# Two f steps of a dense layer in one PSUM bank, with one 512-column activation chain, and an attention operand rebuilt without copies across partitions

## Chip, cores and metric

One core of a Trainium2 chip. The metric is the device time of one execution in microseconds (us); for the kernel before it is the median of three runs. PE is TensorE, DVE VectorE, ACT ScalarE, POOL GpSimd and SP SyncE, which here only issues DMAs.

## The reference, cut to what matters

```python
def reference(q, k, v, n_sink, window, moe, moe2):        # q, k, v: 4 x 8 x 768 x 64
    scores = matmul(q, k.T) / sqrt(64)                     # sliding window of 128 keys and 4 sink keys
    x = matmul(softmax(where(keep, scores, -1e9)), v)      # -> x: 3072 tokens x 512
    h = x @ w_in                                           # first layer: 512 -> 2048
    x = (h - tanh(h)) @ w_out                              # 2048 -> 512
    logits = x @ w_gate + modality_bias[modality_id]       # second layer: 8 experts, one a token
    e = argmax(logits)
    out = gate[e] * (relu(x @ w1[e]) @ w2[e])
```

All in fp32. The kernel computes most products with matmul operands of the type fp32r, in which a number is carried as two parts: hi (the number rounded by a cast) and lo (the number less hi). A product then takes three matmuls, hi·hi, hi·lo and lo·hi.

## The kernel before, in words

The 3072 tokens are worked in 12 **chunks** c of 256. A chunk has 8 **units** U of attention (one per head, 96 in all); the first 14 units (`nf=14`) run in plain fp32, the others with split operands. The first layer ("the first MoE" of the change's description, although it is dense) has 16 **f steps** a chunk, each for 128 of its 2048 inner columns. After it the chunk is routed, and when all chunks are done the second layer runs over 13 pages of 256 tokens of one expert each (the lines from L720 on, `m_...`).

Everything runs in one interleaved stream: while PE works on the first layer of chunk c, the attention of chunks further on is fed in between. The order comes from `run_chunks` (L831): every piece of work is an event with a planned time in units of one f step, `emit` sorts the events, and Tile's scheduler then orders the instructions of each engine, starting from that list. The offsets stand in `self.o` (L45): `lag` (L2's delay behind L1 of the same f), `tg` (gact's delay), `ts` (a_split's) and so on.

The pieces that matter here:

- **L1** (L164): 12 matmuls of 128x256 into one PSUM tile h of one f step. The h tiles come from a pool of two PSUM banks (512 fp32 columns each; before, 256 of them are used).
- **gact** (L177): from h the value g = h − tanh(h), as h·h²·(polynomial in h²). On ACT u = h² (L184) and y = (K1·u + K0)² (L185), on DVE z = u·h (L188) and z = (y + KC)·z (L194), and on ACT a Relu of u whose running sum in `over` (L189) tells whether h ever left the polynomial's range. In that case the whole computation is redone by `general` and `gact_any`, which does not happen with these inputs.
- **g_split** (L197): hi = cast of z on ACT (L211), lo = z − hi on POOL (L216). The tile g holds both.
- **L2** (L237): 6 matmuls of 128x512 for every f step, with the two halves of g as weights, into the accumulators acc0 and acc1, one PSUM bank each.
- **a_split** (L292): from the loaded q (128 partitions x 256: q's 64 rows twice) the operand A = [hi; lo], the upper 64 partitions holding hi and the lower lo. POOL makes the lower half in place (L300, printed as `A<-q,A`, with `sub`'s line L216), then two DMAs on SP's queue copy the halves of A crosswise into B = [lo; hi] (L301, L302). K = [hi; lo] likewise, its lower half by DVE. The scores (L314, L315) are A·K + B·K, in which all four products appear.
- **a_splitv** (L283): V's hi on ACT, its lo on POOL (`V<-v,V`).
- **r_route** (L656): at the end of each chunk POOL issues two indirect DMAs which scatter the gates and token numbers of 2 x 128 tokens into the DRAM table xs (`xs<-pl,sl`).
- **r_order** (L662): after the last chunk but one and after the last, some 20 small DVE operations decide in which order the pages of the second layer run. Their result is the tile `order`; SP reads it and then issues the loads of the pages' weights (L726, `mr<-in_moe_w_dram`) and tokens.

The lines that matter to the change, as they stand:

```python
nc.scalar.activation(u, h, AF.Square)
nc.scalar.activation(y, u, AF.Square, bias=self.k0, scale=K1)
nc.vector.tensor_mul(z, u, h)
nc.vector.scalar_tensor_tensor(out=z, in0=y, scalar=KC, in1=z, op0=ALU.add, op1=ALU.mult)
...
self.sub(self.e("qlo", U < 16), A[D:], q[D:], f32(A[D:]))
nc.sync.dma_start(f32(Bt[:D]), f32(A[D:]))
nc.sync.dma_start(f32(Bt[D:]), f32(A[:D]))
```

Of the kernel before, what the change touches and what calls it, by code (L numbers as in the profile page):

```python
# [40 lines left out]
class Kern:  # L41
    def __init__(self, tc, a):
        self.tc, self.nc, self.a = tc, tc.nc, a
        self.Wi, self.Wo = {}, {}
        self.o = dict(tc='a', xa='g', mt0=-0.28, gz='v', mxe=11, lx='v', nf=14, efh='a', trc=-14.17, tpf=-1.86, xhi='v', vhi='a', vlo='g', qhi='a', khi='v', sT='a', tr='a', ev='a', glo='g', whi='a', wlo='g', gk=0, wl=-8.54, wls=1.25, wd=-3.86, wds=1.05, wo=1, bs=2, be=3, bE=3, bV=1, bg=2, btr=1, bxt=1, pt={'h': 'h', 's': 'r', 'T': 'r', 'R': 'R', 'x': 'R', 'Q': 'R'}, pb=(('r', 2), ('h', 2), ('R', 2)), tl=-9.97, ts=-5.86, tv=-4.34, tsv=-2.34, tS=-5.24, dS=0.07, tN=-4, dN=0.5, tT=-1.78, dT=0.35, tPV=-0.39, txs=-0.28, tg=0.64, tre=0.05, trl=0.48, trr=3.39, u0=-15.64, g=2, lag=1.96, raw=2, sp=2, ghi='a', qlo='g', klo='v', eh='v', xlo='v', x2=4, me=13, mxl=8.77, mxt=1.5, mlag=1.45, mwl=9.99, mws=3.27, mm=0, ev0='v', ghi0='a', vhi0='a', sT0='a', qhi0='a', xlo0='g', eh0='v', y=2)  # L45
# [130 lines left out]

    def gact(self, c, f):  # L177

        nc = self.nc
# [10 lines left out]
        if self.e("gz", c == 0) == "g":  # L190
            nc.scalar.activation(y, y, AF.Identity, bias=self.kc)
            nc.gpsimd.tensor_mul(z, y, z)
        else:
# [24 lines left out]
    def gact_any(self, c, f):  # L218

        nc = self.nc  # L220
        h = self.h.pop((c, f))[:, :CH]
# [1 line left out]
        u = g.tile([P, CH], F32, tag="u", name=f"u{c}_{f}")
        t = g.tile([P, CH], F32, tag="z", name=f"t{c}_{f}")
        y = g.tile([P, CH], F32, tag="y", name=f"gy{c}_{f}")
        m = g.tile([P, CH], U8, tag="m", name=f"m{c}_{f}")
# [777 lines left out]
```

## Time and profile before

| what | value |
|---|---|
| median of 3 runs (lowest to highest) | 1222.81 us (1222.67 to 1223.86) |
| the profiled execution, its device time | 1225.8 us |
| its span in the trace | 1224.0 us |
| mean granted clock of TensorE, share of full speed | 0.96 |
| busy share of PE, DVE, ACT, POOL | 93%, 72%, 62%, 54% |
| DMA: mean rate, packets | 121 GB/s, 88256 |

The profile is of one execution. The span runs from its first to its last recorded instruction, and the device time has 1.8 us more. "Busy" is the time in which an engine worked on instructions; the remaining time it waited, or issued something that isn't counted. In the rows of groups and of the timelines, `<-ENGINE tile` after an idle time names what ended it. The granted clock is the share of the full 2.4 GHz at which the chip let TensorE run in a stretch (0.5 is its lower level, 1.2 GHz).

### The profile page before, as it was taken

Reading aid. Unit: us, or ns where it says so; the run is one execution under the profiler, and the core shown is the slowest. Engines: PE = TensorE matmul, PEld = TensorE weight load, DVE = VectorE, ACT = ScalarE, POOL = GpSimd, SP = SyncE. Lnnn points to the kernel's source line nnn. Section 1 sums busy time; section 2 is a strip of 40 time slices with the busy share of each in tenths; the row PEclk is TensorE's granted clock in tenths of the full one; section 3 lists DMA queues with packets and bytes.
Section 4 is the critical chain, followed back from the end, with each engine's and each line's share of the span. In section 5 each row is a group of like instructions: output and inputs, shape, how many; then the busy total and the mean of one; then the engine's idle time right before and its main releaser. Section 6 shows DMA issues by size and latency. Waiting matters only on the chain. (4 is left out here: it accounts for less than half of the span.)

```text
span 1224.0 us, 23714 instructions
## 1 busy us (share of the span) xinstructions
PE 1135.9 (93%) x7171; PEld 994.8 (81%) x7171; DVE 885.5 (72%) x2419; ACT 757.4 (62%) x2123; POOL 657.7 (54%) x973
## 2 busy tenths in 40 slices
PE   7879998999899899999899999999798999999993
PEld 3447787988789789989789988988687989999992
DVE  6889896888778687978778887966647566666720
ACT  3445765777577678767577877775726555555620
POOL 4987865777667668767667767763302211211200
PEclk9859998999999899999999999999998999999997
DMA  7654232333323233333333323200909777777500
GB/s 206 203 187 137 75 91 62 102 80 102 60 76 90 71 88 85 98 69 104 60 91 83 104 66 87 81 12 19 343 19 327 238 226 213 222 241 219 168 26 6
DMA packets 88256, 147.98 MB, mean 121 GB/s; under 512 B 18864, under 2 KB 64432, under 8 KB 88112
## 3 DMA queue, kind: packets, MB, share of 16 engines
q1 hardware_dynamic: 83184, 133.16, 37.2%
q0 software_dynamic: 4928, 13.14, 3.0%
q8 instruction: 61, 1.00, 0.4%
q14 instruction: 83, 0.68, 0.2%
HBM read 122.86 MB, written 13.17 MB: 111 GB/s over the span
## 5 line engine op out<-in xcount | busy, mean ns | idle before, releaser
L172 PE MATMUL h<-xt,wi 128*128 128x256 f32 x2304 | 356.1, 290 | 9.9 <-DVE gz L188 9.0
L246 PE MATMUL acc<-wo,g 128*128 128x512 f32 x1152 | 334.5, 407 | 24.0 <-POOL g L216 23.1
L172 PEld LDWEIGHTS h<-xt,wi 128*128 128x128 f32 x2304 | 320.5, 194 | 40.4 <-DVE gz L188 12.4
L246 PEld LDWEIGHTS acc<-wo,g 128*128 128x128 f32 x1152 | 198.6, 192 | 53.1 <-POOL g L216 26.0
L216 POOL TENSOR_TENSOR g<-gz,g 128x256 fp32r<-128x256 f32 x192 | 153.4, 802 | 82.3 <-ACT g L211 78.4
L735 DVE TENSOR_TENSOR ml<-mr,mh 128x1024 fp32r<-128x1024 f32 x104 | 127.9, 1236 | 53.4 <-ACT mh L734 51.8
L778 PE MATMUL mh<-mxt,mh 128*128 128x256 f32 x832 | 157.9, 286 | 3.2 <-DVE mxt L768 2.5
L795 PE MATMUL macc<-mh,mg 128*128 128x512 f32 x416 | 147.9, 401 | 4.3 <-DVE mg L782 4.3
L778 PEld LDWEIGHTS mh<-mxt,mh 128*128 128x128 f32 x832 | 138.1, 193 | 12.1 <-DVE mxt L768 2.9
L189 ACT ACTIVATE u<-u,kt 128x256 f32<-128x256 f32 x192 | 97.8, 509 | 80.2 <-DVE gz L188 73.8
L355 POOL TENSOR_SCALAR_AFFINE_SELECT X<-fl 128x512 fp32r<-128x512 f32 (+1 forms) x192 | 119.2, 643 | 33.6 <-DVE fl L385 24.5
L804 POOL DMA_INDIRECT out_dram<-mo,mi x26 | 28.5, 1096 | 200.2 <-ACT mo L803 196.0
L734 ACT CAST mh<-mr 128x1024 fp32r<-128x1024 f32 x104 | 108.6, 1052 | 40.9 <-PE macc L795 25.2
L188 DVE TENSOR_TENSOR gz<-u,h 128x256 f32<-128x256 f32 x192 | 78.9, 414 | 57.5 <-POOL g L216 34.2
L778 PE MATMUL mh<-mxt,ml 128*128 128x256 f32 x416 | 118.5, 286 | 0.0
L194 DVE SCALAR_TENSOR_TENSOR gz<-gy,gz 128x256 f32<-128x256 f32 x192 | 108.3, 570 | 9.2 <-ACT gy L185 2.7
L328 ACT ACTIVATE e<-e,nm 128x160 f32<-128x160 f32 x192 | 82.0, 427 | 48.0 <-DVE nm L326 46.5
L211 ACT CAST g<-gz 128x256 fp32r<-128x256 f32 x192 | 77.0, 402 | 44.4 <-DVE gz L194 29.7
L337 POOL TENSOR_SCALAR e<-e,sm 128x160 f32<-128x160 f32 x192 | 96.9, 515 | 11.6 <-DVE sm L332 9.6
L216 POOL TENSOR_TENSOR A<-q,A 64x256 fp32r<-64x256 f32 x82 | 69.4, 846 | 56.3 <-issue 14.0
L781 ACT ACTIVATE mg<-mh 128x256 fp32r<-128x256 f32 x104 | 40.3, 387 | 94.2 <-PE mh L778 88.3
L185 ACT ACTIVATE gy<-u,k 128x256 f32<-128x256 f32 x192 | 96.5, 510 | 2.5
(211 smaller groups left out, 2270.5 us busy)
## 6 DMA issues: line engine op xcount, KB each, us to landing
mr<-in_moe_w_dram SPq DMA_DIRECT2D x104, 512.0 KB, 4.7
k<-in_k_dram SPq DMA_DIRECT2D x82, 224.0 KB, 2.7
v<-in_v_dram SPq DMA_DIRECT2D x96, 128.0 KB, 2.3
q<-in_q_dram SPq DMA_DIRECT2D x82, 128.0 KB, 2.2
B<-A SPq DMA_DIRECT2D x164, 64.0 KB, 2.1
rawi<-in_moe_w_in_dram SPq DMA_DIRECT2D x16, 512.0 KB, 5.7
rawo<-in_moe_w_out_dram SPq DMA_DIRECT2D x16, 512.0 KB, 5.6
x2d<-x SPq DMA_DIRECT2D x24, 256.0 KB, 2.2
```

Of the source, the lines that this page charges most:

```text
L172: nc.tensor.matmul(h[:, :CH], w[:, wl, k * P:(k + 1) * P], x[:, xl, k], start=(n == 0), stop=(n == 11))
L185: nc.scalar.activation(y, u, AF.Square, bias=self.k0, scale=K1)
L189: nc.scalar.activation(u, u, AF.Relu, bias=self.kt, accum_out=self.over[:, n:n + 1])
L194: nc.vector.scalar_tensor_tensor(out=z, in0=y, scalar=KC, in1=z, op0=ALU.add, op1=ALU.mult)
L216: (self.nc.vector if eng == "v" else self.nc.gpsimd).tensor_tensor(out=out, in0=a, in1=b, op=ALU.subtract)
L246: nc.tensor.matmul(o, g[:, gl, t * P:(t + 1) * P], w[:, wl], start=(f == 0 and n == 0), stop=(f == NF - 1 and n == 2))
L337: self.nc.gpsimd.tensor_scalar(out=e, in0=e, scalar1=r, scalar2=1.0, op0=ALU.mult, op1=ALU.mult)
L355: self.nc.gpsimd.affine_select(out=out, in_=in_, pattern=[[0, n], [s, P]], base=0, channel_multiplier=-s, compare_op=ALU.is_gt if prev els ...
L734: nc.scalar.copy(hi, r)
L735: nc.vector.tensor_sub(lo, r, f32(hi))
L778: nc.tensor.matmul(h, w[:, k * P:(k + 1) * P], x[:, xl, k], start=(n == 0), stop=(n == 11))
L795: nc.tensor.matmul(self.macc[g][t], gt[:, gl, t * P:(t + 1) * P], w[:, DM:], start=(f == 0 and n == 0), stop=(f == n8 - 1 and n == 2))
```

## The change

Three things change.

1. **A pair of f steps shares a bank.** L1 of an even f takes an h tile and fills its columns 0 to 255, L1 of the odd f after it fills columns 256 to 511. gact runs once for the pair, at 512 columns, planned at the odd step's time plus `tg`. z gets no tile of its own: u·h is written over h in PSUM, and (y + KC)·h goes into y. u has one buffer instead of two. g is one tile of 512 columns for the pair, `over` has half the columns, and gact_any is changed in the same way.
2. **`lag` goes from 1.96 to 3.4**, so L2 of every f step, and what is planned behind it (the evacuation of the accumulators, the routing), is planned 1.44 steps later.
3. **a_split without copies.** A stays [hi; hi], and POOL writes lo = q − hi over all 128 partitions of B = [lo; lo]. The two DMAs a unit are gone (164 of them in all). A·K is then hi·hi + hi·lo and B·K is lo·hi + lo·lo.

```diff
@@ L1
+        if f % 2 == 0:
+            self.h[c, f // 2] = self.ps("h", F32, f"h{c}_{f}")
+        h = self.h[c, f // 2][:, (f % 2) * CH:(f % 2 + 1) * CH]
...
@@ gact, now called with p = f // 2
-        u = g.tile([P, CH], F32, tag="u", name=f"u{c}_{f}")
-        y = g.tile([P, CH], F32, tag="y", name=f"gy{c}_{f}")
+        u = g.tile([P, 2 * CH], F32, tag="u", name=f"u{c}_{p}", bufs=1)
+        y = g.tile([P, 2 * CH], F32, tag="y", name=f"gy{c}_{p}")
         nc.scalar.activation(u, h, AF.Square)
         nc.scalar.activation(y, u, AF.Square, bias=self.k0, scale=K1)
-        z = g.tile([P, CH], F32, tag="z", name=f"gz{c}_{f}")
-        n = c * NF + f
-        nc.vector.tensor_mul(z, u, h)
+        n = c * (NF // 2) + p
+        nc.vector.tensor_mul(h, u, h)
         nc.scalar.activation(u, u, AF.Relu, bias=self.kt, accum_out=self.over[:, n:n + 1])
...
-            nc.vector.scalar_tensor_tensor(out=z, in0=y, scalar=KC, in1=z, op0=ALU.add, op1=ALU.mult)
-        self.g_split(c, f, z)
+        nc.vector.scalar_tensor_tensor(out=y, in0=y, scalar=KC, in1=h, op0=ALU.add, op1=ALU.mult)
+        self.g_split(c, p, y)
@@ g_split
-        gt = self.gp.tile([P, 2, CH], F32R, tag="g", name=f"g{c}_{f}", bufs=self.o["g"])
+        gt = self.gp.tile([P, 2, 2 * CH], F32R, tag="g", name=f"g{c}_{p}", bufs=self.o["g"])
@@ L2
+            q = (f % 2) * CH + t * P
-                nc.tensor.matmul(o, g[:, gl, t * P:(t + 1) * P], w[:, wl],
+                nc.tensor.matmul(o, g[:, gl, q:q + P], w[:, wl],
@@ a_split
         self.cast(self.e("qhi", U < 16), A, q)
-        self.sub(self.e("qlo", U < 16), A[D:], q[D:], f32(A[D:]))
-        nc.sync.dma_start(f32(Bt[:D]), f32(A[D:]))
-        nc.sync.dma_start(f32(Bt[D:]), f32(A[:D]))
+        self.sub(self.e("qlo", U < 16), Bt, q, f32(A))
@@ run_chunks
-                    add(t + f + self.o['tg'], self.gact if banded else self.gact_any, c, f)
+                    if f % 2:
+                        add(t + f + self.o['tg'], self.gact if banded else self.gact_any, c, f // 2)
@@ self.o: lag=1.96 becomes lag=3.4
```

How the order moves, at three places. Lines are those of the kernel in question; a name's number after the last underscore tells nothing.

**POOL, the end of chunk 0's first layer and its scatter** (g1_6 and g1_4 are gact's result for f step 6, or now pair 4, of chunk 1; A23 and B24 are operands of attention units 23 and 24). Before, with the semaphores each instruction waits for (DMASW: DMAs of POOL's own queue; DMAHW: DMAs of SP's queue):

```order
L216 TENSOR_TENSOR g1_6_2376<-gz1_6_2372,g1_6_2376 128x256 [waits Activation_49]
L656 DMA xs_63<-pl_336,sl0_2220 4864x2 [waits DVE_49]
L656 DMA xs_63<-pl_336,sl0_2220 4864x2
L216 TENSOR_TENSOR A23_2479<-q23_2164,A23_2479 64x256 [waits DMAHW0_49,DMASW1_49,DMAHW1_49,DMASW0_49,DMAHW3_49,Activation_49,Pool_49]
L216 TENSOR_TENSOR V20_2346<-v20_2161,V20_2346 128x4x64 [waits PE_49,DMAHW4_49,Activation_49,Pool_49]
L216 TENSOR_TENSOR g1_7_2435<-gz1_7_2431,g1_7_2435 128x256 [waits Activation_49]
L355 AFFINE_SELECT X_173<-fl20_2382 128x512 [waits DVE_49]
```

Changed:

```order
L213 TENSOR_TENSOR g1_4_2363<-gy1_4_2357,g1_4_2363 128x512 [waits Activation_49]
L653 DMA xs_63<-pl_336,sl0_2137 4864x2 [waits DVE_49]
L653 DMA xs_63<-pl_336,sl0_2137 4864x2
L213 TENSOR_TENSOR B24_2407<-q24_2181,A24_2406 128x256 [waits DMAHW5_49,PE_49,Activation_49]
L213 TENSOR_TENSOR V21_2283<-v21_2178,V21_2283 128x4x64 [waits DMAHW7_49,PE_49,Activation_49]
L328 TENSOR_SCALAR sm22_2227<-sm22_2227 128x2 [waits Activation_49]
L352 AFFINE_SELECT X_173<-fl21_2312 128x512 [waits DVE_49,Pool_49]
L352 AFFINE_SELECT X_173<-fl21_2312 128x512 [waits Pool_49]
```

Behind the two scatters stands the subtraction of a_split in both. Before, its list of waits names both DMAs that POOL has just issued; after, it names the load of q, PE and ACT only. At the scatters of the other chunks after the change, too, no subtraction waits for DMASW.

**PE, in the last chunk, where no attention is left** (h11_10 is the h tile of chunk 11, f = 10 and, after the change, 11). Before:

```order
L172 MATMUL h11_8_12915<-xt11_12503,wi8_1050 128x256 x12
L246 MATMUL acc11_0_12601<-wo6_981,g11_6_12853 128x512 x2
L246 MATMUL acc11_1_12602<-wo6_981,g11_6_12853 128x512 x2
L172 MATMUL h11_9_12947<-xt11_12503,wi9_1128 128x256 x12
L246 MATMUL acc11_0_12601<-wo6_981,g11_6_12853 128x512
L246 MATMUL acc11_1_12602<-wo6_981,g11_6_12853 128x512
L246 MATMUL acc11_0_12601<-wo7_1043,g11_7_12904 128x512 x2
L246 MATMUL acc11_1_12602<-wo7_1043,g11_7_12904 128x512 x2
L246 MATMUL acc11_0_12601<-wo7_1043,g11_7_12904 128x512
L246 MATMUL acc11_1_12602<-wo7_1043,g11_7_12904 128x512
L172 MATMUL h11_10_12979<-xt11_12503,wi10_1212 128x256 x12
L246 MATMUL acc11_0_12601<-wo8_1121,g11_8_12936 128x512 x2
```

Changed:

```order
L175 MATMUL h11_10_11594<-xt11_11189,wi10_1154 128x256 x3
L245 MATMUL acc11_0_11305<-wo6_950,g11_3_11538 128x512 x2
L245 MATMUL acc11_1_11306<-wo6_950,g11_3_11538 128x512 x2
L175 MATMUL h11_10_11594<-xt11_11189,wi10_1154 128x256 x9
L175 MATMUL h11_10_11594<-xt11_11189,wi11_1227 128x256 x7
L245 MATMUL acc11_0_11305<-wo6_950,g11_3_11538 128x512
L245 MATMUL acc11_1_11306<-wo6_950,g11_3_11538 128x512
L245 MATMUL acc11_0_11305<-wo7_1011,g11_3_11538 128x512 x3
L245 MATMUL acc11_1_11306<-wo7_1011,g11_3_11538 128x512 x3
L175 MATMUL h11_10_11594<-xt11_11189,wi11_1227 128x256 x5
L175 MATMUL h11_12_11654<-xt11_11189,wi12_1288 128x256 x6
L245 MATMUL acc11_0_11305<-wo8_1077,g11_4_11589 128x512 x2
```

Before, L2 of f = 8 begins behind 36 matmuls after L1 of f = 8: the 24 of L1 of f = 9 and 10 and 12 of L2. After, pair 4's first L2 (f = 8, with g11_4) begins behind 42 matmuls after the pair's last of L1, which stands just ahead of these rows: 30 of L1 (f = 10 and 11 and half of f = 12) and 12 of L2 of pair 3.

**DVE, the end of r_order's first call**, which runs in the last chunk on the routing up to chunk 10 (`order_343` is the table of pages, here its first three; gz, or now h and gy, are gact's two DVE operations). Before:

```order
L683 SCALAR_TENSOR_TENSOR olrk_13493<-olsel_13492 128x19
L695 TENSOR_TENSOR oepv_12775<-oepv_12775,pexp_341 128x57
L699 CAST order_343<-oeres_12778 1x3
L684 TENSOR_TENSOR olrk_13493<-olrk_13493,olsel_13492 128x19
L696 TENSOR_REDUCE oeres_12778<-oepv_12775 128x3
L699 CAST order_343<-oeres_12778 1x3
L188 TENSOR_TENSOR gz11_9_12964<-u11_9_12960,h11_9_12947 128x256
L194 SCALAR_TENSOR_TENSOR gz11_9_12964<-gy11_9_12961,gz11_9_12964 128x256
L188 TENSOR_TENSOR gz11_10_12996<-u11_10_12992,h11_10_12979 128x256
L194 SCALAR_TENSOR_TENSOR gz11_10_12996<-gy11_10_12993,gz11_10_12996 128x256
L745 CAST mi0_12869<-mpl0_12867 128x2
```

Changed:

```order
L696 CAST order_343<-oeres_11468 1x3
L681 TENSOR_TENSOR olrk_12115<-olrk_12115,olsel_12114 128x19
L693 TENSOR_REDUCE oeres_11468<-oepv_11465 128x3
L189 TENSOR_TENSOR h11_8_11543<-u11_4_11582,h11_8_11543 128x512
L696 CAST order_343<-oeres_11468 1x3
L191 SCALAR_TENSOR_TENSOR gy11_4_11583<-gy11_4_11583,h11_8_11543 128x512
L189 TENSOR_TENSOR h11_10_11594<-u11_5_11642,h11_10_11594 128x512
L742 CAST mi0_11505<-mpl0_11503 128x2
```

Before, the second write to `order_343` stands ahead of gact of f = 9; after, it stands between the two DVE operations of pair 4, which is f = 8 and 9.

## Rows read from the trace of the kernel before

**Rows 1.** The profile's page, part 1: busy time, share and instructions of each engine

```profile
PE 1135.9 (93%) x7171; PEld 994.8 (81%) x7171; DVE 885.5 (72%) x2419; ACT 757.4 (62%) x2123; POOL 657.7 (54%) x973
```

**Rows 2.** Stretches (us): length, busy us and instructions by engine, clock, DMA

```profile
190.72:792.74 602.02, 571.57 (x3864) 521.92 (x3863) 481.59 (x1539) 428.06 (x1389) 416.25 (x665) 0.97 0.32 83
467.10:527.92 60.82, 60.54 (x424) 55.79 (x423) 51.87 (x167) 46.47 (x152) 46.63 (x73) 1.00 0.33 91
```

**Rows 3.** POOL in order of time: start, length, operation [idle before <-releaser]

```profile
192.25 0.98 POOL L656 DMA_INDIRECT xs<-pl,sl  x1 [0.30 <-issue]
199.49 0.72 POOL L216 TENSOR_TENSOR A<-q,A 64x256 fp32r<-64x256 f32 x1 [6.26 <-DMA k<-in_k_dram]
...
264.24 0.97 POOL L656 DMA_INDIRECT xs<-pl,sl  x1 [0.30 <-issue]
265.22 0.74 POOL L216 TENSOR_TENSOR g<-gz,g 128x256 fp32r<-128x256 f32 x1
...
798.86 0.73 POOL L216 TENSOR_TENSOR A<-q,A 64x256 fp32r<-64x256 f32 x1 [2.95 <-PE s L315]
```

**Rows 4.** DMA issues: tiles, queue, count, KB, median us to landing

```profile
xs<-pl,sl POOLq DMA_INDIRECT x24, 4.7
B<-A SPq DMA_DIRECT2D x164, 64.0 KB, 2.1
```

**Rows 5.** PE waits, 190 to 800, then 790 to 815: us, times, longest

```profile
PE acc L246 <- POOL g L216: 21.0, 7, 5.6
PE R L413 <- POOL V L216: 4.6, 2, 2.3
...
PE acc L246 <- POOL g L216: 1.4, 1, 1.4
```

**Rows 6.** The stretch after the first of these waits, columns as in rows 2

```profile
202.00:210.00 8.00, 8.00 (x36) 7.15 (x37) 5.99 (x16) 5.05 (x17) 5.97 (x11) 0.69 0.30 86
```

**Rows 7.** Groups by line and shape: busy us, mean ns | idle before, releasers

```profile
L184 ACT ACTIVATE u<-h 128x256 f32<-128x256 f32 x192 | 71.1, 378 | 28.9 <-PE h L172 28.4
L185 ACT ACTIVATE gy<-u,k 128x256 f32<-128x256 f32 x192 | 96.5, 510 | 2.5
L188 DVE TENSOR_TENSOR gz<-u,h 128x256 f32<-128x256 f32 x192 | 78.9, 414 | 57.5 <-POOL g L216 34.2 <-ACT u L184 22.6
L194 DVE SCALAR_TENSOR_TENSOR gz<-gy,gz 128x256 f32<-128x256 f32 x192 | 108.3, 570 | 9.2 <-ACT gy L185 2.7 <-DVE gz L188 0.9
L211 ACT CAST g<-gz 128x256 fp32r<-128x256 f32 x192 | 77.0, 402 | 44.4 <-DVE gz L194 29.7 <-PE acc L246 6.7 <-POOL g L216 1.6
L216 POOL TENSOR_TENSOR g<-gz,g 128x256 fp32r<-128x256 f32 x192 | 153.4, 802 | 82.3 <-ACT g L211 78.4
L211 ACT CAST wi<-yi 128x512 fp32r<-128x512 f32 x16 | 9.9, 620 | 14.2 <-DVE yi L148 14.2
L216 POOL TENSOR_TENSOR wi<-yi,wi 128x512 fp32r<-128x512 f32 x16 | 23.9, 1491 | 3.5 <-ACT wi L211 3.1
```

**Rows 8.** The first MoE's end in order of time: PE, then SP's queue

```profile
854.76 2.00 PE L246 MATMUL acc<-wo,g 128*128 128x512 f32 x8
856.60 1.60 PE L172 MATMUL h<-xt,wi 128*128 128x256 f32 x12
858.03 1.09 PE L246 MATMUL acc<-wo,g 128*128 128x512 f32 x4
882.29 0.38 PE L778 MATMUL mh<-mxt,mh 128*128 128x256 f32 x1 [2.28 <-DVE mxt L768]
...
856.80 2.42 SPq L726 DMA_DIRECT2D mr<-in_moe_w_dram  x2
```

**Rows 9.** PE in the start-up, chunk 0

```profile
85.25 2.93 PE L172 MATMUL h<-xt,wi 128*128 128x256 f32 x12 [2.96 <-DVE gz L188]
```

**Rows 10.** VectorE's K residue, once alone and once beside a POOL subtraction

```profile
191.24 0.62 DVE L216 TENSOR_TENSOR K<-k,K 64x448 fp32r<-64x448 f32 x1
206.00 1.08 DVE L216 TENSOR_TENSOR K<-k,K 64x448 fp32r<-64x448 f32 x1
```

More of the change, by code (lines that the diff above doesn't have):

```diff
@@ L44, in __init__ @@
         self.Wi, self.Wo = {}, {}
[L45 removed]
+        self.o = dict(tc='a', xa='g', mt0=-0.28, gz='v', mxe=11, lx='v', nf=14, efh='a', trc=-14.17, tpf=-1.86, xhi='v', vhi='a', vlo='g', qhi='a', khi='v', sT='a', tr='a', ev='a', glo='g', whi='a', wlo='g', gk=0, wl=-8.54, wls=1.25, wd=-3.86, wds=1.05, wo=1, bs=2, be=3, bE=3, bV=1, bg=2, btr=1, bxt=1, pt={'h': 'h', 's': 'r', 'T': 'r', 'R': 'R', 'x': 'R', 'Q': 'R'}, pb=(('r', 2), ('h', 2), ('R', 2)), tl=-9.97, ts=-5.86, tv=-4.34, tsv=-2.34, tS=-5.24, dS=0.07, tN=-4, dN=0.5, tT=-1.78, dT=0.35, tPV=-0.39, txs=-0.28, tg=0.64, tre=0.05, trl=0.48, trr=3.39, u0=-15.64, g=2, lag=3.4, raw=2, sp=2, ghi='a', qlo='g', klo='v', eh='v', xlo='v', x2=4, me=13, mxl=8.77, mxt=1.5, mlag=1.45, mwl=9.99, mws=3.27, mm=0, ev0='v', ghi0='a', vhi0='a', sT0='a', qhi0='a', xlo0='g', eh0='v', y=2)
     def e(self, k, start):
@@ L171, in L1, with gact, g_split @@
             for wl, xl in ((0, 0), (0, 1), (1, 0)):
-                nc.tensor.matmul(h[:, :CH], w[:, wl, k * P:(k + 1) * P], x[:, xl, k],
+                nc.tensor.matmul(h, w[:, wl, k * P:(k + 1) * P], x[:, xl, k],
                                  start=(n == 0), stop=(n == 11))
                 n += 1
-        self.h[c, f] = h
-    def gact(self, c, f):
+    def gact(self, c, p):
         nc = self.nc
-        h = self.h.pop((c, f))[:, :CH]
+        h = self.h.pop((c, p))
         g = self.gp
-        u = g.tile([P, CH], F32, tag="u", name=f"u{c}_{f}")
-        y = g.tile([P, CH], F32, tag="y", name=f"gy{c}_{f}")
+        u = g.tile([P, 2 * CH], F32, tag="u", name=f"u{c}_{p}", bufs=1)
+        y = g.tile([P, 2 * CH], F32, tag="y", name=f"gy{c}_{p}")
         nc.scalar.activation(u, h, AF.Square)
         nc.scalar.activation(y, u, AF.Square, bias=self.k0, scale=K1)
-        z = g.tile([P, CH], F32, tag="z", name=f"gz{c}_{f}")
-        n = c * NF + f
-        nc.vector.tensor_mul(z, u, h)
+        n = c * (NF // 2) + p
+        nc.vector.tensor_mul(h, u, h)
         nc.scalar.activation(u, u, AF.Relu, bias=self.kt, accum_out=self.over[:, n:n + 1])
[L190 to L193, printed above, removed]
-            nc.vector.scalar_tensor_tensor(out=z, in0=y, scalar=KC, in1=z, op0=ALU.add, op1=ALU.mult)
-        self.g_split(c, f, z)
-    def g_split(self, c, f, z):
+        nc.vector.scalar_tensor_tensor(out=y, in0=y, scalar=KC, in1=h, op0=ALU.add, op1=ALU.mult)
+        self.g_split(c, p, y)
+    def g_split(self, c, p, z):
         nc = self.nc
-        gt = self.gp.tile([P, 2, CH], F32R, tag="g", name=f"g{c}_{f}", bufs=self.o["g"])
+        gt = self.gp.tile([P, 2, 2 * CH], F32R, tag="g", name=f"g{c}_{p}", bufs=self.o["g"])
         self.cast(self.e("ghi", c == 0), gt[:, 0], z)
         self.sub(self.e("glo", c == 0), gt[:, 1], z, f32(gt[:, 0]))
-        self.g[c, f] = gt
+        self.g[c, p] = gt
     def ps(self, kind, dt, name):
@@ L216, in sub, with gact_any @@
         (self.nc.vector if eng == "v" else self.nc.gpsimd).tensor_tensor(out=out, in0=a, in1=b, op=ALU.subtract)
-    def gact_any(self, c, f):
+    def gact_any(self, c, p):
         nc = self.nc
-        h = self.h.pop((c, f))[:, :CH]
+        h = self.h.pop((c, p))
         g = self.gp
[L223 to L226, printed above, removed]
+        w = 2 * CH
+        u = g.tile([P, w], F32, tag="u", name=f"u{c}_{p}", bufs=1)
+        t = g.tile([P, w], F32, tag="z", name=f"t{c}_{p}")
+        y = g.tile([P, w], F32, tag="y", name=f"gy{c}_{p}")
+        m = g.tile([P, w], U8, tag="m", name=f"m{c}_{p}")
         nc.scalar.activation(u, h, AF.Square)
@@ L234, in gact_any @@
         nc.vector.copy_predicated(u, m, h)
-        self.g_split(c, f, u)
+        self.g_split(c, p, u)
     def L2(self, c, f):
@@ L240, in L2 @@
             self.acc[c] = [self.psa.tile([P, DM], F32, tag=f"a{t}", name=f"acc{c}_{t}") for t in range(CH // P)]
-        g, w = self.g.pop((c, f)), self.Wo[f]
+        g, w = self.g[c, f // 2], self.Wo[f]
         for t in range(CH // P):
             o = self.acc[c][t]
+            q = (f % 2) * CH + t * P
             n = 0
             for gl, wl in ((0, 0), (0, 1), (1, 0)):
-                nc.tensor.matmul(o, g[:, gl, t * P:(t + 1) * P], w[:, wl],
+                nc.tensor.matmul(o, g[:, gl, q:q + P], w[:, wl],
                                  start=(f == 0 and n == 0), stop=(f == NF - 1 and n == 2))
@@ L531, in r_consts @@
         self.npi = cp.tile([1, 1], I32, name="npi")
-        self.over = cp.tile([P, NCH * NF], F32, name="over")
+        self.over = cp.tile([P, NCH * NF // 2], F32, name="over")
         self.k0 = cp.tile([P, 1], F32, name="k0")
```

1 line of the change is left out of this document (removed).

## The prediction

> **What bounds the kernel now.** I read the page's part 1 first: PE is busy in 1135.9 of 1224.0 us, 93% [rows 1], so either matmuls go away or the missing 7% and the clock come back. The change removes no matmul. The next view is the table of stretches [rows 2]. A chunk in the middle (467 to 528 us) takes 60.82 us, of which PE is busy for 60.54, at a granted clock of 1.00: there PE alone sets the pace, and nothing done on ACT, DVE or POOL can help. But over 190.72 to 792.74 us, ten chunks' stretch with the same kind of work, PE is busy for 571.57 of 602.02 us at a clock of 0.97. The question is what separates that long stretch from the middle chunk.
>
> The waits of PE name it: of the 30.45 us of idle, 25.6 were ended by POOL, 21.0 by g's subtraction (7 waits, up to 5.6 us) and 4.6 by V's [rows 5]. POOL's own timeline shows where it lost the time [rows 3]. At 192.25 a scatter is issued for 0.98 us, then POOL stands still for 6.26 us until `A<-q,A` starts at 199.49. There are seven such gaps, the last at 798.86 (2.95 us). At 264.24, where g's subtraction comes next in order instead of A's, it starts without any gap. The profile prints k's load or PE as the releaser of the gaps, but in the order of before the subtraction behind a scatter lists the two DMAs POOL has just issued (DMASW) among its waits. A scatter takes 4.7 us to land, a copy `B<-A` 2.1 [rows 4]: gaps of 3 to 6 us fit the scatter. So a subtraction that has nothing to do with routing waits for the routing's scatter, and g's and V's subtractions queue behind it on POOL; PE waits for those. The clock follows: in 202 to 210, behind the first gap, PE is busy for all of 8.00 us at 0.69 and does only 36 matmuls [rows 6], while the middle chunk's rate gives 56 in 8 us. The clock is thus part of the price of a gap.
>
> **The change part by part.**
>
> *a_split.* Without the in-place A and its two DMAs, B's subtraction waits for q's load, PE and ACT in the order of after, and at no chunk for DMASW. The price of the gaps: one matmul of the middle chunk costs 60.82/424 = 0.1434 us, so the 3864 matmuls of the long stretch should take 554.3 us, and it took 602.0: 47.7 us are lost. A second way agrees: 30.45 of idle and 0.03 x 602 = 18 of clock are 48.5. Not all is due to the gaps: 30.45 − 25.6 = 4.9 us of idle have other releasers, while the middle chunk's idle of 0.28 scaled to 602 us is 2.8; so 2 us stay. The seventh gap lies beyond the stretch, with a PE wait of 1.4 us [rows 5]: 1 us. Gain: 47.7 − 2 + 1 = **46.7 us**. The 164 DMAs lie on SP's queue under work of PE and are counted at nothing. B's subtraction has 128 partitions instead of 64 at the same 256 columns; A's took 0.72 to 0.73 [rows 3], g's of 128 partitions 0.74 at 265.22, so it costs nothing on POOL.
>
> *One chain for a pair.* At 256 columns the chain from h to hi is 0.378 (u) + 0.510 (y, under which DVE's 0.414 lies) + 0.570 (second DVE operation) + 0.402 (cast) = 1.86 us, and 0.80 on POOL to lo [rows 7]. At 512 columns the upper bound is twice that, 3.72. The lower takes 512-column rows: wi's cast, 0.62, for u and for the cast, and for each of DVE's two K's residue scaled from 448 columns, 0.71 [rows 10]: 2.66. I take 3.0 as between; lo adds 1.49 (wi's subtraction of 512), 4.5 in all, at most 5.2. What covers it: PE's work between a pair's last L1 matmul and its first L2. In the last chunk, the leanest, these are 30 matmuls of L1 and 12 of L2. One of L1 costs 1.43/12 = 0.119 us (856.60 to 858.03), one of L2 1.84/8 = 0.23 (854.76 to 856.60) [rows 8]: 3.6 + 2.8 = 6.3 us, and the lo part is wanted four matmuls of L2 and two of L1 later, at 7.5. So 3 us are spare, about as before (24 of L1 and 12 of L2: 5.6 us against 1.86). With attention in between, an f step takes 60.82/16 = 3.8 us instead of 2.8, and the cover is longer. Counted at **nothing**; were it gone, the rival below shows the price. ACT and DVE have less to do (192 chains become 96 of less than twice the length), but both are covered by PE.
>
> *Start-up.* In chunk 0 there is no L2 yet between L1s, and PE waited 2.96 us for DVE's gz at 85.25 [rows 9]. A pair holds its bank until the second DVE operation has read it, and the fifth L1 is the first that waits for a bank now. Bounds: all of the 2.96 gone, and some 4 us more by less work on ACT and DVE there; or a chain longer by 3.0 − 1.86 = 1.1 and once more 0.8 on POOL, 1.9 lost. The rows are nearest to a small gain: **1 us**.
>
> *The end of the first layer.* The second write to `order_343` moves from ahead of gact of f = 9 to between pair 4's DVE operations. The weights' loads start from it (SP at 856.80), and the first page's matmul comes at 882.29 after a PE wait of 2.28 [rows 8], so this chain of 25.5 us ends last there. Lag is up by 1.44 steps of 2.8 us: 4 us later; less DVE work ahead of it gives some 2 back. I take a loss of **2 us**, bounds 0 and 8 (two steps and the 2.28).
>
> Sum, against the profiled execution's 1225.8: 1225.8 − 46.7 − 1 + 2 = 1180.1. The median of the runs is 3.0 below that execution, so **1177** on the median's scale.
>
> **The rivals.**
>
> *1. POOL's longer subtractions hold DVE up* (0.15). K's residue took 0.62 us alone and 1.08 at 206.00 beside a POOL subtraction [rows 10]: 0.46 more. A g subtraction is now one of 1.49 instead of two of 0.80, so a DVE operation caught behind it can lose up to 0.7 more at once. If each of some 80 K residues loses another 0.46, that is 37 us of DVE time; DVE is busy for 46.47 us of the middle chunk's 60.82 [rows 2], so I let under half of it reach PE: 15 us, 1192, between 1184 and 1200. Against it: the second DVE operation (0.570 on average) now reads h from PSUM and only y from SBUF, and u·h, which already does so, took 0.414 [rows 7]. The Trainium skill's page "SBUF — State Buffer" (section "SBUF: two separate sides") says that DVE and GpSimd share a port pair as an exclusive lock for the whole instruction, taken by a DVE operation with two SBUF inputs only against a GpSimd one that reads SBUF. By that rule the second DVE operation escapes and K's residue does not; rows 10 agree in direction, and no row shows how often it happens with 1.49.
>
> *2. The chain outruns its cover: slower* (0.04). PE would then wait once for every pair, 96 times, and at 0.8 us each that is 77 us: 1177 + 77 = 1254. It is slower than before from 46/96 = 0.5 us a pair on. For it: ACT is also asked by attention and DVE is at 76% in the middle chunk, so a chain can queue; against it: it would need over 3 us of queueing for every pair, and with one buffer of u and two banks of h there is no more slack than that.
>
> *3. The wait moves to another instruction* (0.04). The scatter is still on POOL's queue; if what stands behind it waited for its landing all the same, nothing would be gained: 1222. Against it is the order's list of waits.
>
> *4. More comes back* (0.05). With no clock drop at chunk ends and the start-up's better bound (7 us), 1166 or below.
>
> **How the numbers follow.** The forecast (gaps gone, cover holds) has 0.72, with 1168 to 1186 of its own: the end's 8 instead of 2 and start-up's −1.9 instead of +1 are 9 up, the start-up's best and the end's 0 are 8 down. With rival 1 the range reaches 1193, and with part of rival 4 down to 1166; outside lie rivals 2 and 3, most of 4 and the top of 1, under 0.2. A difference of 0.2%, 2.4 us, is about what a measurement of this kernel can tell from none. Faster by more: forecast and rivals 1 and 4, 0.92; within: rival 3, 0.04; slower: rival 2, 0.04.
>
> **What would show it.** Right: no POOL gap behind a scatter, no acc wait of PE on g over 2 us between 190 and 800, each chunk near 61 us at a clock of 0.99 or more. The 512-column ACT operations should take 0.6 to 1.0 us and g's subtraction 1.5. Rival 1 would show as a DVE mean for K's residue well above 0.62 with PE waiting on DVE; rival 2 as dozens of PE waits on g of about the same length; a later end as a first page matmul more than 26 us behind the weights' load or that load later against L2's end. It is wrong if the gaps are gone and the middle stretches still run at 65 us a chunk: then something else sets the clock.

## The result, and the profile after

| kernel | median (lowest to highest) | span of the profiled execution | granted clock |
|---|---|---|---|
| before, four runs beside the changed kernel | 1223.34 us (1222.67 to 1224.69) | 1224.0 us | 0.96 |
| changed, four runs | 1184.09 us (1183.02 to 1188.39) | 1182.6 us | 0.98 |

The ratio is 0.9684, with a 95% interval of 0.9659 to 0.971: faster by 3.2%, or 39 us. The forecast was 1177 us, within 1166 to 1193.

The table of stretches, first: the changed kernel over the same 3863 matmuls as the long stretch of [rows 2] (PE's 766th to 4629th, for every kernel in what follows), and then over those of the middle chunk. Behind the length stand the busy time and the instructions of PE, of PE's weight loads, of DVE, ACT and POOL in this order, then the granted clock, the DMA engines' busy share and GB/s.

```profile
191.34:754.20 562.86, 557.48 (x3869) 512.82 (x3867) 461.83 (x1392) 378.29 (x1029) 394.57 (x593) 1.00 0.26 72
442.88:503.47 60.59, 60.17 (x424) 55.16 (x423) 49.59 (x158) 41.62 (x113) 43.85 (x67) 1.00 0.27 75
```

The long stretch is 39.2 us shorter (602.02 before). Its idle time of PE, length less the first busy figure, fell from 30.45 to 5.38 us, and the clock is back at 1.00. The middle chunk took 60.82 and takes 60.59: nothing was gained where nothing stood still. The profile's time thus went where it was sought: the start up to that stretch takes 0.6 us more (191.34 for 190.72), and what follows the stretch 3 us less, about half of it the seventh gap of [rows 3], the only one that lies behind the stretch.

POOL behind the first scatter, in order of time, the rows that answer to [rows 3]:

```profile
200.83 1.26 POOL L653 DMA_INDIRECT xs<-pl,sl  x1 [0.32 <-DVE s L316]
202.40 0.98 POOL L653 DMA_INDIRECT xs<-pl,sl  x1 [0.30 <-issue]
203.39 0.77 POOL L213 TENSOR_TENSOR B<-q,A 128x256 fp32r<-128x256 f32 x1
204.09 0.76 POOL L213 TENSOR_TENSOR V<-v,V 128x256 fp32r<-128x256 f32 x1
```

The subtraction for B starts 0.01 us behind the scatter's issue, where A's stood still for 6.26. PE's waits from 190 to 800 us (time in all, how often, longest), all that the view lists, answer to [rows 5]:

```profile
PE h L175 <- DVE gy L191: 1.8, 8, 0.4
PE h L175 <- DVE xt L210: 1.3, 3, 0.4
PE s L311 <- DVE sT L383: 0.9, 1, 0.9
PE s L311 <- DVE nm L323: 0.7, 1, 0.7
```

The 25.6 us that POOL ended are gone. What the view lists now is 4.7 us, all of it ended by DVE; eight of the waits, 0.4 us at most, are for the pair's second DVE operation, which frees a bank of h. The groups of the new chain, to set against [rows 7]; the row of `K<-k,K` stands here for after and, under it, for before:

```profile
L186 ACT ACTIVATE u<-h 128x512 f32<-128x512 f32 x96 | 56.3, 586 | 30.8 <-PE h L175 30.2
L187 ACT ACTIVATE gy<-u,k 128x512 f32<-128x512 f32 x96 | 69.3, 722 | 2.5
L189 DVE TENSOR_TENSOR h<-u,h 128x512 f32<-128x512 f32 x96 | 66.0, 687 | 21.2 <-ACT u L186 19.5 <-issue 0.9
L191 DVE SCALAR_TENSOR_TENSOR gy<-gy,h 128x512 f32<-128x512 f32 x96 | 65.5, 682 | 3.2
L208 ACT CAST g<-gy 128x512 fp32r<-128x512 f32 x96 | 59.2, 617 | 16.5 <-DVE gy L191 10.3 <-PE acc L245 5.6
L213 POOL TENSOR_TENSOR g<-gy,g 128x512 fp32r<-128x512 f32 x96 | 132.4, 1379 | 63.0 <-ACT g L208 60.3 <-PE T L345 0.8 <-PE acc L245 0.6
L213 DVE TENSOR_TENSOR K<-k,K 64x448 fp32r<-64x448 f32 x82 | 85.1, 1038 | 2.7
```

```profile
L216 DVE TENSOR_TENSOR K<-k,K 64x448 fp32r<-64x448 f32 x82 | 68.1, 830 | 2.6
```

From h to hi the chain takes 0.586 + 0.722 + 0.682 + 0.617 = 2.61 us, with u·h under y, and 1.38 more to lo.

### The profile page after: what moved, and what is told of

The parts are those of the page before. It is cut to its first block, busy times and chain, and to the rows that moved or that the text cites. A ratio compares the mean times of both kernels' runs of the same rounds, so it can differ in the third digit from the quotient of the medians.

```text
span 1182.6 us, 22303 instructions
## 1 busy us (share of the span) xinstructions
PE 1118.5 (95%) x7171; PEld 984.5 (83%) x7171; DVE 860.0 (73%) x2227; ACT 689.8 (58%) x1643; POOL 636.3 (54%) x877
## 5 line engine op out<-in xcount | busy, mean ns | idle before, releaser
L175 PEld LDWEIGHTS h<-xt,wi 128*128 128x128 f32 x2304 | 313.1, 193 | 30.1 <-DVE xt L210 5.8
L245 PE MATMUL acc<-wo,g 128*128 128x512 f32 x1152 | 313.6, 399 | 5.1 <-POOL g L213 3.5
L213 POOL TENSOR_TENSOR g<-gy,g 128x512 fp32r<-128x512 f32 x96 | 132.4, 1379 | 63.0 <-ACT g L208 60.3
L190 ACT ACTIVATE u<-u,kt 128x512 f32<-128x512 f32 x96 | 69.5, 723 | 44.5 <-DVE h L189 23.3
L334 POOL TENSOR_SCALAR e<-e,sm 128x160 f32<-128x160 f32 x192 | 88.5, 472 | 9.7 <-DVE sm L329 8.0
L792 PEld LDWEIGHTS macc<-mh,mg 128*128 128x128 f32 x416 | 77.9, 190 | 18.1 <-DVE mg L779 5.3
L213 POOL TENSOR_TENSOR B<-q,A 128x256 fp32r<-128x256 f32 x82 | 71.5, 871 | 39.1 <-ACT A L208 38.2
L213 DVE TENSOR_TENSOR K<-k,K 64x448 fp32r<-64x448 f32 x82 | 85.1, 1038 | 2.7
L213 POOL TENSOR_TENSOR V<-v,V 128x256 fp32r<-128x256 f32 x82 | 65.0, 793 | 35.3 <-ACT V L208 35.2
L792 PE MATMUL macc<-ml,mg 128*128 128x512 f32 x208 | 82.4, 396 | 0.0
```

Of the source, the lines that this page charges most:

```text
L175: nc.tensor.matmul(h, w[:, wl, k * P:(k + 1) * P], x[:, xl, k], start=(n == 0), stop=(n == 11))
L213: (self.nc.vector if eng == "v" else self.nc.gpsimd).tensor_tensor(out=out, in0=a, in1=b, op=ALU.subtract)
L245: nc.tensor.matmul(o, g[:, gl, q:q + P], w[:, wl], start=(f == 0 and n == 0), stop=(f == NF - 1 and n == 2))
L334: self.nc.gpsimd.tensor_scalar(out=e, in0=e, scalar1=r, scalar2=1.0, op0=ALU.mult, op1=ALU.mult)
L792: nc.tensor.matmul(self.macc[g][t], gt[:, gl, t * P:(t + 1) * P], w[:, DM:], start=(f == 0 and n == 0), stop=(f == n8 - 1 and n == 2))
```

## The experiments

The kernels of one call ran on one chip, beside runs of the kernel before. There were several chips, and the kernel before ran at 1223 us on the first and at 1213 to 1215 on the others, so each verdict is against its own chip.

**1. Part 3 of the change alone.**

```diff
-        self.sub(self.e("qlo", U < 16), A[D:], q[D:], f32(A[D:]))
-        nc.sync.dma_start(f32(Bt[:D]), f32(A[D:]))
-        nc.sync.dma_start(f32(Bt[D:]), f32(A[:D]))
+        self.sub(self.e("qlo", U < 16), Bt, q, f32(A))
```

> The kernel before with part 3 of the change alone: B's subtraction over 128 partitions on POOL, no copies; single f steps of 256 columns and lag 1.96 stay. Theory (the wait for the scatter costs nearly all of it, the pair and the lag nothing): no POOL gap behind a scatter, no PE wait on g over 2 us between 190 and 800 us, clock 1.00 there, 1184 us (1179 to 1190), as the full change. Rival (the pair's shorter work on ACT and DVE gives a good part): 1200 us or more. Rival (the removed wait only moves): 1219 to 1226 us.

1183.69 us against 1215.39 (ratio 0.9743, 0.9718 to 0.9769). The long stretch:

```profile
189.04:752.99 563.95, 557.75 (x3865) 510.97 (x3863) 483.74 (x1542) 427.54 (x1389) 420.18 (x665) 1.00 0.27 72
```

563.95 us, 6.2 of them idle on PE, at 1.00: within 1.1 us of the full change, although ACT works for 427.54 us instead of 378.29. The theory holds, and the pair with its lag adds nothing to it. The scatters still take long to land: behind the first chunk the second one was issued at 190.63 and landed 6.3 us later, and B's subtraction did not wait for that.

```profile
190.63 0.98 POOL L654 DMA_INDIRECT xs<-pl,sl  x1 [0.30 <-PE h L172]
191.61 0.78 POOL L216 TENSOR_TENSOR B<-q,A 128x256 fp32r<-128x256 f32 x1
```

**2. The change without part 3** (the three lines of a_split as before, put into the changed kernel).

> The change without its part 3: pairs of 512 columns, z in place and lag 3.4, but A's subtraction in place and the two copies, as before. In its order an A subtraction that waits for the scatter stands directly behind it at seven of nine scatters and behind one other instruction at two; before, of ten, two stood directly, five behind one, three far off. Theory: all nine gaps of POOL are 4 to 7 us long, each costs 6 to 7 us (40 us for six of before's), so 1184 + 9 x 6.6 = 1243 us (1225 to 1255), slower than before. Rival (the pair gives a good part): under 1215 us. Rival (the gaps of before are bound to the shorter lag): 1184 to 1200 us.

1210.64 us against 1215.39 (0.9965, 0.995 to 0.9981), and the 1243 us were missed. By the number alone the first rival (under 1215 us) came true; the trace, of the slowest of the ten runs, decides against it. The theory's place was right and its price wrong. The long stretch takes 590.38 us, and nine gaps behind scatters stand in it, the first of them here:

```profile
194.48:784.86 590.38, 565.25 (x3869) 517.87 (x3867) 457.11 (x1392) 378.27 (x1029) 391.72 (x593) 0.99 0.31 85
```

```profile
204.39 1.26 POOL L655 DMA_INDIRECT xs<-pl,sl  x1 [0.33 <-DVE s L318]
205.96 0.98 POOL L655 DMA_INDIRECT xs<-pl,sl  x1 [0.30 <-issue]
210.15 0.72 POOL L213 TENSOR_TENSOR A<-q,A 64x256 fp32r<-64x256 f32 x1 [3.21 <-issue]
```

Seven of the nine are 2.9 to 3.2 us long, one is 5.65 and one 1.81, 28.9 us in all; against the changed kernel's stretch 27.5 us are lost, so the pair gives nothing beyond the shorter gaps. A gap costs about its length, and the length is no constant, as taken for the 1243 us. The view of the tile xs gives the landing of these two scatters, and under it that of the first two of the kernel before (shortest, median, longest, in us):

```profile
DMA to landing us min/median/max: 3.9/4.2/4.5
```

```profile
DMA to landing us min/median/max: 5.1/6.0/6.9
```

The second scatter is the one of 3.9 us here and the one of 6.9 before. Its issue at 205.96 plus 3.9 us brings 209.9, and A's subtraction starts at 210.15; before, it was 192.25 plus 6.9, 199.15, and the subtraction started at 199.49 [rows 3]. The gap is the time to the landing. The other traces say the same: in the kernel before (on both chips of experiment 8), in this one and in those of experiments 3 and 6, 34 gaps stand in front of such a subtraction, and each ends 0.29 to 0.63 us after the second scatter has landed, whatever releaser the profile names. What makes a landing short or long stayed open.

**3. One copy instead of two, and no subtraction in place.**

```diff
-        self.sub(self.e("qlo", U < 16), A[D:], q[D:], f32(A[D:]))
-        nc.sync.dma_start(f32(Bt[:D]), f32(A[D:]))
-        nc.sync.dma_start(f32(Bt[D:]), f32(A[:D]))
+        self.sub(self.e("qlo", U < 16), Bt[D:], q[D:], f32(A[D:]))
+        nc.sync.dma_start(f32(Bt[:D]), f32(Bt[D:]))
```

> The kernel before with A = [hi; hi], POOL's subtraction for the lower 64 partitions of B alone and one copy (lower half of B to its upper half) instead of two. The subtraction is not in place any more, but a copy that reads what it writes is left, and its list of waits still holds the scatters, at the same ten places as before. Theory (the wait for the scatter is what costs): 1222 us (1217 to 1227). Rival (half of the cost is the copies' load on SP's queue and the DMA rings): about 1203 us. Rival (being in place is what costs): 1184 us.

1215.97 us against 1215.39 (1.0011, 0.999 to 1.0031): no difference. Here the profile names the releaser itself:

```profile
192.76 0.98 POOL L655 DMA_INDIRECT xs<-pl,sl  x1 [0.30 <-issue]
199.94 0.72 POOL L216 TENSOR_TENSOR B<-q,A 64x256 fp32r<-64x256 f32 x1 [6.20 <-DMA xs<-pl,sl]
```

**4. The same copy behind a subtraction over all 128 partitions.**

```diff
-        self.sub(self.e("qlo", U < 16), Bt[D:], q[D:], f32(A[D:]))
+        self.sub(self.e("qlo", U < 16), Bt, q, f32(A))
         nc.sync.dma_start(f32(Bt[:D]), f32(Bt[D:]))
```

> The kernel before with B's subtraction over all 128 partitions, as the change has it, but with the copy of one_copy kept (lower half of B onto its upper half, which holds the same numbers already). Against one_copy only the number of partitions of POOL's subtraction differs, 128 for 64. In the order the wait for the scatters is gone. Theory (the wait comes with the subtraction over half the partitions, not with copies): no POOL gap behind a scatter, 1184 us (1180 to 1190). Rival (copies that read and write B cost the time): 1210 us or more, as one_copy.

1185.03 us against 1214.78 (0.9755, 0.9733 to 0.9776). Set against the kernel of experiment 3, the edit above changes the subtraction alone. Behind the first scatter:

```profile
191.98 0.98 POOL L655 DMA_INDIRECT xs<-pl,sl  x1 [0.30 <-PE h L172]
192.95 0.78 POOL L216 TENSOR_TENSOR B<-q,A 128x256 fp32r<-128x256 f32 x1
```

A copy a unit stays and costs next to nothing. Experiments 3 and 4 differ in one thing, 64 or 128 partitions in POOL's subtraction, and that takes the ratio, each to its own chip's kernel before, from 1.0011 to 0.9755: with the half, the list of waits that the scheduler writes for it names the scatters, with the whole it doesn't. Why the scheduler does so was not pursued, and whether it is the size of the half that counts or its start at partition 64 was not separated.

**5. The kernel before without its scatters** (`for t in range(NTL)` around them becomes `range(0)`).

> The kernel before without the scatters of the routing (left out: the table of tokens and gates is never filled, so the second layer writes no row of the output); copies, in-place subtraction and order of the rest stay. What counts is how far PE is at the end of the attention. Theory (the gaps are waits for the scatters' landing): no POOL gap over 3 us between 190 and 800 us, clock 1.00 there, and PE's 4600th matmul at 749 us as in split_only, where before had it at 780 to 789. Rival (the subtraction waits for k's load or the copies, as the profile's releasers say): the gaps stay, 775 us or later.

In one run PE's 4600th matmul starts at 754 us, between the theory's 749 and the 775 from which the rival held, and the long stretch is

```profile
190.88:758.09 567.21, 559.94 (x3864) 514.12 (x3863) 480.03 (x1542) 427.63 (x1389) 395.22 (x647) 0.99 0.31 88
```

567.2 us, where the kernel before takes 594 to 602, with copies and in-place subtraction all there. POOL still stands still for over 3 us at two places (285.68 and 797.72), both ended by ACT. So the scatters are what is waited for; the copies leave waits of 2 us on POOL (V's subtraction at 193.58 waited 2.11 for B's copy) that hardly reach PE. The total of 1172.08 says nothing, since the second layer writes no rows.

**6. The routing half a step later** (`trr=3.39` becomes `3.9`).

> The kernel before with one number changed: trr 3.39 becomes 3.9, so that the routing with its scatters is planned half a step later; copies and waits all stay. In the order three A subtractions that wait for a scatter stand directly behind it (chunks 0, 2 and the last), the other seven behind four to eight instructions, where before seven stood within one. Theory: POOL gaps at three places alone, four of before's gone at about 6.6 us each: 1222.8 - 26 = 1197 us (1190 to 1206). Rival (the scatter isn't what the gaps wait for): 1219 to 1226 us.

1212.06 us against 1215.39 (0.9982, 0.996 to 1.0004): no difference by that interval, and a miss. The long gaps are where the theory put them, at 198.39 (5.43 us), 329.22 (5.92) and 783.45 (3.29); at a fourth place the subtraction, five instructions behind its scatter, still waited for the landing:

```profile
467.37 0.84 POOL L216 TENSOR_TENSOR A<-q,A 64x256 fp32r<-64x256 f32 x1 [2.08 <-ACT e L328]
```

But in the long stretch

```profile
190.38:777.35 586.97, 565.86 (x3865) 514.57 (x3863) 477.39 (x1542) 427.75 (x1390) 413.56 (x665) 0.99 0.31 85
```

23.0 us more are lost than in split_only's, and the three gaps in it (13.4 us) can carry about two thirds at the price that experiment 8 gives. The rest are many waits under 1.5 us around the later routing; the longest were ended by DVE's `xt` (1.43) and POOL's `e` (0.95). A move of the routing thus takes most of the gaps away and pays for it elsewhere, and what exactly it pays for stays open.

**7. Two half subtractions, no copies** (the edit as set against the kernel of experiment 1).

```diff
-        self.sub(self.e("qlo", U < 16), Bt, q, f32(A))
+        self.sub(self.e("qlo", U < 16), Bt[D:], q[D:], f32(A[D:]))
+        self.sub(self.e("qlo", U < 16), Bt[:D], q[:D], f32(A[:D]))
```

> The kernel before with B's subtraction on POOL as two instructions of 64 partitions each, no copies. The order has the wait for the scatters on the lower half's subtraction, as before, but at seven or more of ten places five to nine instructions behind the scatter; at one it is one and at one two behind. One more POOL instruction of 0.7 us a unit. Theory (the wait comes with half-partition subtractions and costs only where it stands near the scatter): one or two gaps, 1184 + 2 x 3 = 1190 us (1183 to 1198). Rival (the wait costs wherever it stands): 1212 us or more.

1230.82 us against 1212.66 (1.0148, 1.0117 to 1.0179): slower than the kernel before, the clearest miss. The gaps went as the theory had it: in the long stretch there is one of over 3.4 us behind a scatter (3.97 us at 677.24). The rival's number came true (1212 or more), but of POOL's idle time in front of these subtractions, 35.8 us, the profile puts only 4.6 down to the scatters. What the theory left out is the added work on POOL:

```profile
192.42:800.00 607.58, 576.69 (x3865) 516.76 (x3865) 502.16 (x1529) 428.85 (x1387) 470.92 (x734) 0.99 0.24 67
```

```profile
L216 POOL TENSOR_TENSOR B<-q,A 64x256 fp32r<-64x256 f32 x164 | 135.6, 827 | 35.8 <-ACT A L211 9.8 <-DMA xs<-pl,sl 4.6 <-issue 3.9
```

and, for the changed kernel,

```profile
L213 POOL TENSOR_TENSOR B<-q,A 128x256 fp32r<-128x256 f32 x82 | 71.5, 871 | 39.1 <-ACT A L208 38.2 <-PE h L175 0.7
```

A subtraction over 64 partitions takes 0.83 us and one over 128 takes 0.87, so the second half costs a whole one, 64 us of POOL in all. POOL is then busy for 471 of 608 us, and the stretch is 43.6 us longer than split_only's, spread over all chunks. So 64 us of added work on POOL were not free, although POOL had been idle for 46% of the span before. The way to PE is only in part POOL's own: of PE's waits between 192 and 800 us POOL ended 11.8 us and DVE 17.3; the longest of each kind in all are

```profile
PE s L313 <- DVE nm L325: 6.4, 10, 1.0
PE T L346 <- POOL e L336: 4.1, 6, 1.7
```

DVE is busy for 502 us where it was for 484 in split_only. Besides, PE's busy time for the same matmuls is 576.69 instead of 557.75 us at a clock of 0.99; what makes it so long was not looked into.

**8. Both kernels on another chip.**

> The kernel before, unchanged, for a trace from the same chip as the three kernels with it. The chip of the first experiments ran it at 1215 us, the first chip at 1223. Theory: the same seven gaps of POOL behind scatters, but shorter by the scatters' landing time, 32 us in all between 190 and 800 us instead of 40. Rival: the gaps cost the same and the difference lies in the start-up.

> The changed kernel, unchanged. Theory (it has no gap, so nothing of the chip's scatter time shows): 1184 us (1181 to 1188) on whichever chip, level with split_only's 1183.7. Rival (this chip is faster by 8 us for every kernel): 1176 us.

1214.64 us, and 1183.76 against 1214.78 (0.9762, 0.9732 to 0.9791). The first gap and the two long stretches, before and changed:

```profile
198.28 0.72 POOL L216 TENSOR_TENSOR A<-q,A 64x256 fp32r<-64x256 f32 x1 [5.95 <-DMA k<-in_k_dram]
```

```profile
189.74:783.84 594.10, 568.44 (x3865) 518.84 (x3864) 482.95 (x1543) 426.48 (x1389) 417.99 (x665) 0.98 0.32 84
```

```profile
189.59:752.37 562.78, 557.39 (x3868) 512.77 (x3866) 461.79 (x1392) 378.18 (x1029) 394.37 (x593) 1.00 0.26 72
```

The changed stretch is the same to 0.1 us on both chips, and before's is 8.0 us shorter here. Its six gaps add up to 28.0 us instead of 33.6 on the first chip (32 for 40 were expected), for 31.3 us lost instead of 39.2: 1.12 and 1.17 us for each us of a gap. The chip's difference is in the gaps, as the theory has it, and the change is worth 31 us on one chip and 39 on another for that reason.

**9. Pairs with the old lag** (`lag=3.4` back to `1.96` in the changed kernel).

> The changed kernel with lag 1.96 as before. In its order the first L2 of pair 4 in the last chunk stands behind 17 matmuls of L1 after the pair's last, instead of 30. Theory (the cover was longer than the chain by 3 us, so the lag isn't needed): cover 17 x 0.119 + about 12 x 0.23 = 4.8 us against a chain of 2.6 us (0.586 + 0.687 + 0.682 + 0.617 as the changed kernel's rows have it): 1184 us (1180 to 1192). Rival (the lag carries the pair): PE waits on g once a pair for half a microsecond or more, 1230 us and above.

1199.40 us against 1214.78 (0.9872, 0.9848 to 0.9895): between the theory's 1184 and the rival's 1230, so both are missed. PE's waits from 190 to 800 us, the six longest:

```profile
PE s L311 <- DVE nm L323: 3.5, 6, 0.9
PE h L175 <- DVE gy L191: 2.9, 6, 1.2
PE h L175 <- DVE xt L213: 2.9, 7, 1.1
PE s L311 <- DVE sT L383: 2.1, 4, 0.7
PE h L175 <- DVE xt L210: 1.5, 3, 0.5
PE acc L245 <- POOL g L213: 0.7, 3, 0.3
```

```profile
188.83:767.43 578.60, 563.63 (x3866) 514.70 (x3864) 464.11 (x1398) 379.69 (x1032) 393.57 (x594) 0.99 0.25 70
```

The cover of L2 held, as the theory said: waits on g are 0.7 us for lo and 0.3 for hi. But PE is idle for 15.0 us instead of 5.4, in front of L1 (a bank of h not yet read by `gy`, a late `xt`) and of the scores, and the clock follows. The lag gives back 15.6 us that the pair costs without it; the pair and the lag together come out at nothing. The lag alone, without the pair, was not run.

**10. A try for more: fewer plain units** (`nf=14` to 12, and to 10, in split_only).

> An attempt at a faster kernel: split_only with 12 instead of 14 units of plain fp32 at the start. Two units less in four-pass fp32 on PE, two units more of casts and subtractions on ACT, POOL and DVE in the start-up, where copies don't delay B any more. If PE's fp32 matmuls limit the start-up: 1180 us; if DVE's work there does (its slices are at 9 and 8 tenths): 1184 to 1190 us.

> As split_nf12 with 10 plain units, one look: twice its difference to split_only's 1183.7 us, in the same direction.

1188.69 us against 1212.66 (0.9789, 0.9761 to 0.9817) and, in one run, 1196.13: 5 and 12 us behind split_only, which ran on another chip (ratio 0.9743); the first is the expectation's second case. The long stretch takes 564.0 us with 12 plain units, as in split_only, and starts at 196.78 instead of 189.04, so the loss lies in the start-up. The plain units at the start are worth keeping. No kernel here beats the changed one; split_only is level with it.

## Why the prediction was right, and where its sizes were off

- **The bound and the cause** held. What could be had of the 7% that PE lacked was the wait behind the scatters: of PE's 88 us of idle time 24 are gone, and of the 64 that stay all but 5.4 lie before the long stretch and behind it. Nearly all of the gain lies in the long stretch: the middle chunk stands, most of the idle time is gone, the clock is at 1.00. Part 3 alone gives it (experiment 1).
- **Readings that were wrong** without changing the sum: the 46.47 us of the middle chunk, and the 76% made of them, are ACT's; DVE was busy for 51.87 us, 85% [rows 2], so rivals 1 and 2 had less room on DVE than they reckoned with. The long stretch runs from the first to the tenth chunk's scatter and is nine chunks long, not ten. The forecast's own range, 8 us below 1177, begins at 1169 and not 1168.
- **What makes the wait** was put more broadly than it is. The prediction laid it to the subtraction in place and its two DMAs; experiments 3, 4 and 5 leave the half of the partitions as the feature that counts, and the scatter's landing as what is waited for.
- **The sum's large term, 46.7 us, was too large.** The two medians differ by 39.2 us where 45.7 were forecast. Of the term, 45.7 belong to the long stretch, which gave 39.2. The step that failed is the yardstick, one matmul of the middle chunk at 0.1434 us as the pace of the whole stretch. With nothing standing still, the long stretch takes 557.48/3869 = 0.1441 us of PE's busy time a matmul, but the middle chunk 60.17/424 = 0.1419, 1.5% or 8 us in 557, against the 6.5 us by which the stretch missed. The middle chunk is one of the quick ones. In split_only, without a gap, the 422 matmuls that start in it take

```profile
441.50:502.06 60.56, 60.29 (x424) 55.75 (x422) 51.65 (x167) 46.54 (x151) 45.42 (x73) 1.00 0.27 75
```

  and 422 of the long stretch 61.6 us on average (563.95 x 422/3863), in runs of 422 one behind the other between 60.7 and 63.6. Some 2 us of the 6.5 come from the division by 424, which counts two matmuls that the window's edges cut. Where the rest comes from stays open; it is not the kind of matmul, for those of 512 columns, the longest, are 22% in the middle chunk of the kernel before as in its whole stretch. The cross-check that agreed (30.45 of idle and 18 of clock) was too large too: 25.1 us of idle went (5.4 stay), and PE's busy time fell by 14.1, less than the 18 that the rounded clock of 0.97 gave.
- **The chain of a pair** was taken as 3.0 and 4.5 us and is 2.61 and 3.99, just below the lower bounds of 2.66 and 4.15. Its cover held: PE's waits on g between 190 and 800 us are gone; at the very end, where no L1 is left to cover it, it did not (under "the end"). "Counted at nothing" was right for the pair with its lag, but only for both together: experiment 9 shows the lag carrying 15.6 us, through the banks of h and `xt`, which the prediction hadn't costed.
- **Start-up**: −1 forecast, +0.6 measured up to PE's 766th matmul in the profile. The wait of [rows 9] is gone, but the scores' waits on DVE's `nm` grew from 2.1 to 10.4 us; the sum stays inside the bounds.
- **The end**: +2 forecast, some 1.5 us gained measured, outside the bounds of 0 and 8. The step that failed is the one that put the page's weights 4 us later. Counted from the end of the long stretch, their load comes 62.5 us behind it (816.69) where it came 64.1 behind (856.80), so it is 1.6 us earlier; why the lag does not show there was not looked into. The first page's matmul was misread too: it stands at 879.47 in the kernel before, ahead of the wait of 2.28 on `mxt` [rows 8], which does not come back.

```profile
879.47 0.53 PE L778 MATMUL mh<-mxt,mh 128*128 128x256 f32 x2
```

  Changed: POOL, PE, then SP's queue:

```profile
833.20 1.70 POOL L750 DMA_INDIRECT mx<-x2d,ms  x1 [4.97 <-ACT mh L731]
835.21 1.95 POOL L750 DMA_INDIRECT mx<-x2d,ms  x1 [0.30 <-issue]
837.18 1.28 POOL L213 TENSOR_TENSOR g<-gy,g 128x512 fp32r<-128x512 f32 x1
...
833.76 1.20 PE L245 MATMUL acc<-wo,g 128*128 128x512 f32 x4 [1.42 <-ACT g L208]
838.51 3.44 PE L245 MATMUL acc<-wo,g 128*128 128x512 f32 x8 [3.12 <-POOL g L213]
841.78 0.52 PE L775 MATMUL mh<-mxt,mh 128*128 128x256 f32 x3
...
816.69 2.61 SPq L723 DMA_DIRECT2D mr<-in_moe_w_dram  x2
```

  The load at 816.69 is 25.1 us ahead of the first page's matmul (22.7 before), which follows an L2 without a wait. PE now waits for g instead: 1.42 us for hi and 3.12 for lo of the last pair but one. That lo, at 837.18, stood in POOL's queue behind the issue of two gathers for the second layer.
- **Rival 1** had its mechanism and not its price. K's residue went from 0.830 to 1.038 us on average, 17 us of DVE's time, and PE's waits on DVE between 190 and 800 us are 4.7 us in all. The trace shows the mechanism by itself: a residue that started while POOL was idle took 0.62 us in both kernels, one that started under g's subtraction 0.89 on average before (14 of them) and 1.55 after (15). The second DVE operation escaped: 0.682 us for 512 columns, as u·h (0.687), where it took 0.570 for 256 [rows 7]. This is what the Trainium skill's page "SBUF — State Buffer", section "SBUF: two separate sides", lets one expect of an operation that has one input in PSUM; the rows agree with it.
- **Rivals 2, 3 and 4** didn't come. Rival 3 was the right one to keep: in experiment 2 the rest of the change leaves the wait where it was, and even brings a subtraction close behind nine of the scatters.
